# Scaling w_sp on ScalarE and taking a quarter of z2 in seven block products

## The chip, the cores and the metric

The kernel runs on one core of a Trainium2 chip. The metric is the device time of one execution in microseconds; the median of three runs of the kernel before is 669.81 us (669.75 to 670.06). The profile is of one further execution. TensorE (PE in the profile) multiplies, VectorE (DVE) and ScalarE (ACT) work on tiles of 128 partitions, GpSimd (POOL) does little here, and SyncE (SP) issues all DMAs from one queue.

## The reference

Two branches read the same x (2048 x 1024, bf16) and a gate mixes them.

```
g = sigmoid((x * gate_w).sum(-1))
# branch A: 32 heads of 32, each position looks at 8 positions back, 2 apart
q, k, v = x @ wqkv
a = softmax(q . k[pos - 2w], w = 0..7) . v  @ wo
# branch B
z  = gelu(x @ w_in)              # 2048 x 3584
z1 = z[:, :1792]
z2 = layernorm(z[:, 1792:])
gg = w_sp @ z2 + b_sp            # w_sp is 2048 x 2048
b  = (z1 * gg) @ w_out
out = g * a + (1 - g) * b
```

## The kernel before

Many large products are made as seven block products instead of eight: the operands are cut in four blocks, sums of blocks are formed beforehand (`s1` to `s4` on the left, `t1` to `t4`, `r1` to `r4` and so on at the right), and TensorE's accumulation in two banks with copies in between gives the four result blocks. For this the operands are float16, scaled by powers of two so that they fit: x by `xs`, the upper half of w_in's z2 columns by `dsc`, each row of w_sp by `rs` (a power of two from the row's sum of absolute values, `l1`), and so on. The scale is taken out again where the result leaves PSUM.

The kernel is written out in one order by hand. A small planner (`Beat`) counts the columns that TensorE has been given, at 2360 columns a microsecond, and calls functions that were booked for a time (`beat.at`) when that time is passed; it also books the steps of the attention on VectorE one behind the other (`vector_steps`). What it fixes is only the order of instructions on each engine; on the chip the engines wait for each other by semaphores.

The stages, in the order of TensorE's work, with the profile's times:

- Start (0 to 49 us): x comes in, the first two tiles turned by TensorE, the others by DMA transposes. z2's lower half (columns 0 to 895, `w2`, in two parts c = 0 and 1 of 448 columns) is made for the first 8 of 16 row tiles in plain tiles: `z2_tile` is 8 matmuls of 448 columns (line 374). Between them lie the projections of head group 0: `qkv_tile` is 8 matmuls of 384 columns (line 947). When x's sum of absolute values is known (`x_abs`, `x_total`, `x_scale`, line 401), x is turned to float16 in place (`x_convert`).
- Head groups 1 and 2 (to 94 us), while ScalarE and VectorE prepare the upper half of the columns (`d_norm`, `d_convert`, `d_sum`) and x's block sums (`x_sums`).
- Eight block groups (`z2_group`, line 455; 94 to 178 us): the upper half of z2's columns (c = 2 and 3, 449 columns with one for the gate) for all rows, 256 rows each, seven products of four matmuls; four projection tiles of head groups 3 and 4 stand among them. In two free slots of each group ScalarE takes what is held back: an exponential of the attention, a sum of the output, or a square sum of z2 (`squares`, line 1023).
- Head groups 5 to 7 (178 to 266 us), 48 projection tiles, with the remaining 16 plain tiles of z2's lower half, rows 1024 to 2047, among them. ScalarE forms the row sums of w_sp (`row_norm`, line 767) from natural rows.
- z1 (266 to 363 us): four parts of 448 columns by 16 tiles (line 1098). VectorE normalises z2 and forms the sums of its blocks (line 808).
- The mix (363 to 534 us): w_sp times z2 in 16 groups (`g_group`, line 1115), eight pairs of 256 rows, an even and an odd group for the two halves of the columns, each seven products of eight matmuls. The rows of w_sp come by DMA transpose (`load_rows`, line 792) into the buffer of the next pair, VectorE scales them (`scale_rows`, line 799; the scale lies along the free dimension after the transpose, so it is stored to DRAM and loaded back broadcast to all partitions, line 795), then forms the block sums (`s_sums`). ScalarE takes the seed copy (line 1139), p5 (line 1125), u2 and u3 (line 1127), the copy of the seed (line 1161) and the last block (line 1177). Beside that it scales y of the pair before in odd groups (`y_scale_beside`, line 912), sums it (`y_norm`, line 894), and in spare slots (`spare`) takes an output sum (line 688) or a chunk of wo (`wo_norm`, line 865).
- The products with wo and w_out (534 to 669 us).

Of the kernel before, what the change touches and what calls it, by code (L numbers as in the profile page):

```python
# [48 lines left out]
ARENA = R_OFF + 36864  # L49
# [3 lines left out]
T4_OFF = R_OFF + 21760  # L53
G_OFF = R_OFF + 28928
SN_OFF = R_OFF + 32512
# [7 lines left out]
def kernel(  # L63
# [34 lines left out]
    rs_d = dpool.tile([S], BF, name="rs_d")  # L98
# [21 lines left out]
    rs_b = sm.tile([P, 512], BF, name="rs_b")  # L120
# [5 lines left out]
    rows_one = rs_b[:, 0:P]  # L126
# [17 lines left out]
    rs_r = sm.tile([16, P], BF, name="rs_r")  # L144
# [12 lines left out]
    x_sc = sm.tile([P, 4], F32, name="x_sc")  # L157
    xs, xinv, xexp, xsum = [x_sc[:, m:m + 1] for m in range(4)]
# [19 lines left out]
    w2 = reg(R_OFF + 7168, KT * W2P).rearrange("p (k c) -> p k c", k=KT)  # L178
# [7 lines left out]
    r1 = z2f[:, 8:12, 0:DN]  # L186
    r2, r4 = [reg(R_OFF + 3072 + 4 * DN * r, 4 * DN).bitcast(F16).rearrange("p (k n) -> p k n", k=4) for r in range(2)]
    r3 = m12
    x_waste = reg(Z_OFF, 16 * FH).rearrange("p (i f) -> p i f", i=16)[:, 8:12, 0:DN]

    class Tokens:
        def __init__(self, u):
# [6 lines left out]
            if u < 7:  # L199
                self.s4 = z2f[:, 12:16, P * u:P * u + P]  # L200
            else:
                self.s4 = reg(R_OFF + 33922, 512).bitcast(F16).rearrange("p (k t) -> p k t", t=P)
# [10 lines left out]
    junk = reg(R_OFF + 33024, 2048)  # L213
# [9 lines left out]
    class Pair:  # L223
        def __init__(self, off):
            v = [reg(off + 1024 * r, 1024).bitcast(F16).rearrange("p (k t) -> p k t", k=8) for r in range(7)]
            both = reg(off, 4096).rearrange("p (h i t) -> p h i t", h=2, i=16)
            self.raw = [both[:, 0], both[:, 1]]
            both = reg(off, 4096).bitcast(F16).rearrange("p (h i t) -> p h i t", h=2, i=16)
            self.scaled = [both[:, 0], both[:, 1]]
# [10 lines left out]
    rs_bc = [rs_b[:, 256 * r:256 * (r + 1)] for r in range(2)]  # L240
# [127 lines left out]
    def z2_block(blocks, wake=False):  # L368
        banks = [seeded.tile([P, 512], F32, name="sd", tag="sd") if wake else bank() for _ in blocks]
        for kt in range(KT):  # L370
            for ps, (i, c) in zip(banks, blocks):
# [3 lines left out]
                                 _sub_ap(w2, kt * W2P + ZC * c, [[1, N]]),  # L375
                                 start=(kt == 0), stop=(kt == KT - 1), skip_group_check=wake)
        for ps, (i, c) in zip(banks, blocks):
            scale = xinv if converted[i // 2] else 1.0
            z2_out(ps[:, 0:ZC], i, c, scale)
            beat.run(KT * ZC)  # L380
# [18 lines left out]
    def x_scale():  # L399
        ps = psum.tile([P, 512], F32, name="ps", tag="ps")  # L400
        nc.tensor.matmul(ps[:, 0:1], rows_one, rs_n[:, 0:1], start=True, stop=True)
        powers(ps[:, 0:1], xs, xinv)
        nc.vector.tensor_scalar(xexp, xinv, xinv, float(SCALE), ALU.mult, ALU.mult)

# [3 lines left out]
    def x_sums(u):  # L408
# [5 lines left out]
        TT(v.s4, v.a12, v.s2, ALU.subtract)  # L414
        beat.on_vector(1.5)
# [30 lines left out]
    def z2_keep(ps):  # L446
        out = z2_snaps[z2_kept[0] % 5]
        z2_kept[0] += 1
        nc.scalar.copy(out, ps[:, 0:DN - 1])
        return out  # L450
# [964 lines left out]
```

## Time and profile before

| | us |
|---|---|
| median of three runs | 669.81 |
| profiled execution | 671.13 |
| its span, first to last instruction | 669.3 |
| TensorE busy | 662.7 |
| VectorE busy | 575.1 |
| ScalarE busy | 441.9 |
| granted TensorE clock | 1.00 |

A row of the timeline gives the start of an instruction or a run of equal ones, its length, engine, line, what it writes and reads, and in brackets how long the engine sat idle ahead of it and what ended that. Matmuls are pipelined: one of 448 columns is shown with 0.35 us, but eight of them follow in 1.51 us, and the chain of waits shows this pace.

### The profile page before, as it was taken

The numbers are of one execution on the slowest core, as the hardware profiler recorded it, in microseconds if no ns is written. First come the engines' busy times: TensorE is split into PE (matmuls) and PEld (weight loads), VectorE is DVE, ScalarE is ACT, GpSimd is POOL, SyncE is SP. The second block draws the span as 40 slices with busy tenths as digits, with TensorE's granted clock in tenths as the row PEclk, the third lists the DMA queues.
The fourth block names the chain that finished last, engine by engine and source line by source line (L and its number), as shares of the span: only waits on it lengthen the run. The fifth ranks groups of instructions, "written<-read, shape, count | busy, mean of one in ns | idle before, by whom it ended". The sixth has DMA issues, their size and how long they took to land.

```text
span 669.3 us, 9594 instructions
## 1 busy us (share of the span) xinstructions
PE 662.7 (99%) x3564; PEld 389.3 (58%) x3564; DVE 575.1 (86%) x660; ACT 441.9 (66%) x774; POOL 9.4 (1%) x68
## 2 busy tenths in 40 slices
PE   8999999999999999999999999999999999999998
PEld 4558877666777777555555555555555544444443
DVE  4567999999999999999999999999978788954745
ACT  4327577888879989889755568787767774522222
POOL 0000000000001000001000000000000000000000
PEclk9999999999999999999999999999999999999999
DMA  8999593354297996994966686648589599476211
GB/s 224 182 235 255 113 227 116 105 121 120 45 283 244 279 290 203 280 327 150 292 207 213 154 217 161 166 116 229 131 211 288 142 270 225 85 167 151 54 63 64
DMA packets 229919, 123.92 MB, mean 185 GB/s; under 512 B 191088, under 2 KB 217456, under 8 KB 229872
## 3 DMA queue, kind: packets, MB, share of 16 engines
q1 hardware_dynamic: 229872, 123.31, 69.7%
q8 instruction: 28, 0.46, 0.3%
q14 instruction: 19, 0.16, 0.1%
HBM read 63.97 MB, written 37.82 MB: 152 GB/s over the span
## 4 chain that ended last, share of the span: by engine, by line
PE 97%; ACT 1%; DMA 1%; SPq 0%; issue 0%; DVE 0%
PE ps L1115 25%; PE ps L947 17%; PE pd L1115 12%; PE ps L1098 7%; PE seed L1115 7%; PE sd L947 5%; PE pd L374 4%; PE ps L455 4%; PE sd L1098 4%; PE pd L1098 4%; PE pd L947 2%; PE pd L455 2%; PE ps L374 1%; PE sd L374 1%; PE seed L455 1%; DMA arena<-in_B_w_in_dram 1%
## 5 line engine op out<-in xcount | busy, mean ns | idle before, releaser
L1115 PEld LDWEIGHTS <-arena 128*128 128x128 f16 x1519 | 148.4, 98 | 154.4 <-issue 0.7
L1115 PE MATMUL ps<-arena 128*128 128x448 f16 (+1 forms) x864 | 186.1, 363 | 0.2 <-ACT seed L1139 0.2
L947 PEld LDWEIGHTS <-arena 128*128 128x128 f16 (+1 forms) x1024 | 141.6, 139 | 30.4 <-issue 1.2
L947 PE MATMUL ps<-arena 128*128 128x384 bf16 x704 | 128.7, 326 | 0.0
L1115 PE MATMUL pd<-arena 128*128 128x448 f16 (+1 forms) x432 | 95.6, 363 | 0.0
L1098 PEld LDWEIGHTS <-arena 128*128 128x128 f16 x512 | 50.0, 98 | 46.7
L514 DVE TENSOR_TENSOR arena<-arena 128x4096 bf16<-128x4096 bf16 (+1 forms) x64 | 74.0, 1157 | 1.7
L510 DVE TENSOR_TENSOR arena<-arena 128x8192 bf16<-128x8192 bf16 x16 | 70.8, 4422 | 5.0 <-DMA arena<-k_d 4.7
L577 DVE TENSOR_TENSOR arena<-arena,att_A 128x8192 bf16<-128x8192 bf16 x16 | 70.7, 4421 | 0.2
L950 ACT CAST arena<-ps 128x384 bf16<-128x384 f32 x88 | 43.0, 489 | 23.6 <-PE ps L947 21.4
L1098 PE MATMUL ps<-arena 128*128 128x448 bf16 x256 | 53.7, 353 | 0.0
L1115 PE MATMUL seed<-arena 128*128 128x448 f16 (+2 forms) x223 | 48.7, 361 | 0.0
L947 PE MATMUL sd<-arena 128*128 128x384 bf16 x224 | 41.0, 326 | 0.8 <-ACT arena L383 0.8
L374 PEld LDWEIGHTS <-arena 128*128 128x128 f16 (+1 forms) x256 | 24.9, 98 | 23.0 <-ACT arena L359 1.1
L583 DVE TENSOR_TENSOR arena<-arena 128x4096 bf16<-128x4096 bf16 x16 | 36.6, 2287 | 0.2
L374 PE MATMUL pd<-arena 128*128 128x448 bf16 x160 | 34.7, 353 | 0.0
L1273 DVE SCALAR_TENSOR_TENSOR arena<-seed,omr,arena 128x512 bf16<-128x512 f32 x8 | 6.0, 751 | 32.7 <-PE seed L1115 32.7
L455 PEld LDWEIGHTS <-arena 128*128 128x128 f16 x224 | 21.9, 98 | 18.1 <-issue 0.5
L767 ACT ACTIVATE arena<-arena 128x2048 bf16<-128x2048 bf16 x16 | 30.9, 1932 | 0.0
L894 ACT ACTIVATE arena<-arena 128x896 bf16<-128x896 bf16 x32 | 30.3, 947 | 0.5
L455 PE MATMUL ps<-arena 128*128 128x449 f16 x128 | 29.7, 354 | 0.0
L387 DVE TENSOR_REDUCE yl<-arena 128x1 f32<-128x2048 bf16 x8 | 18.3, 2286 | 13.1 <-DMA arena<-in_A_x_dram 13.0
(207 smaller groups left out, 845.9 us busy)
## 6 DMA issues: line engine op xcount, KB each, us to landing
arena<-in_B_w_sp_dram SPq DMA_DIRECT2D x16, 512.0 KB, 4.2
arena<-v_d SPq DMA_DIRECT2D x8, 960.0 KB, 6.0
z_d<-arena SPq DMA_DIRECT2D x16, 448.0 KB, 4.5
arena<-z_d SPq DMA_DIRECT2D x16, 448.0 KB, 3.6
y_d<-arena SPq DMA_DIRECT2D x16, 448.0 KB, 4.1
arena<-k_d SPq DMA_DIRECT2D x7, 960.0 KB, 6.7
arena<-in_A_wqkv_dram SPq DMA_DIRECT2D x24, 256.0 KB, 4.6
q_d<-arena SPq DMA_DIRECT2D x32, 128.0 KB, 2.1
```

What stands on the lines that cost most here:

```text
L374: nc.tensor.matmul(ps[:, 0:N], x[:, kt, i * P:(i + 1) * P], _sub_ap(w2, kt * W2P + ZC * c, [[1, N]]), start=(kt == 0), stop=(kt == KT - 1) ...
L455: nc.tensor.matmul(ps[:, 0:DN - 1], lhsT, v[:, k, 0:DN - 1], start=(first and k == 0), stop=(k == 3), skip_group_check=True)
L510: TT(prod.rearrange("p (w j c) -> p w j c", w=W, j=8, c=C), in0, in1, ALU.mult)
L514: return lambda: TT(pv[:, :, 0:n], pv[:, :, 0:n], pv[:, :, n:2 * n], ALU.add)
L577: TT(prod.rearrange("p (w j d h) -> p w j d h", w=W, j=8, d=DH, h=HG), in0, in1, ALU.mult)
L583: return [(4.4, mul), (2.3, lambda: TT(p3[:, 0:4, :], p3[:, 0:4, :], p3[:, 4:8, :], ALU.add)), (1.2, lambda: TT(p3[:, 0:2, :], p3[:, 0:2, ...
L767: nc.scalar.activation(slot, slot, ACT.Abs, accum_out=l1[:, a:a + 1])
L894: nc.scalar.activation(waste, g_ring[n % 4][:, r], ACT.Abs, accum_out=yl[:, k:k + 1])
L947: nc.tensor.matmul(ps[:, 0:3 * C].rearrange("p (t c) -> p t c", t=3), lhsT, wgt[:, :, kt, :], start=(kt == 0), stop=(kt == KT - 1))
L950: nc.scalar.copy(st[:, j % 4, :].rearrange("p (t d h) -> p t d h", t=3, h=HG), ps[:, 0:3 * C].rearrange("p (t h d) -> p t d h", t=3, h=HG))
L1098: nc.tensor.matmul(ps[:, 0:512 if whole and kt == 0 else ZC], xh[:, kt, i * P:(i + 1) * P], _sub_ap(w1, kt * ZC, [[1, 512 if whole and kt ...
L1115: nc.tensor.matmul(ps[:, 0:c1 - c0], w[:, k, :], v[:, k, c0:c1], start=(first and k == 0), stop=(k == K - 1), skip_group_check=True)
```

## The change

Two things change, and much of the order with them.

1. *w_sp is scaled ahead of the transpose.* ScalarE scales natural rows (the scale is then one number per partition) in pieces of 128 rows by 1024 columns (`w_scaled`), the piece is stored to a scratch in DRAM (`w_d`), and the transpose reads that. Rows 0 to 511 go through in z1, eight pieces; the others in the mix, four pieces per pair for two pairs ahead (`w_ahead` loads, `w_piece` scales and books the store). Pieces 0 and 1 use the block-sum buffers of the pair's own buffer, pieces 2 and 3 one buffer, `w_tail`. The scaling on VectorE, the broadcast scales and their DMAs are gone. In `g_group` the pieces take slots that the spare work had, and odd groups get a spare slot behind u2.
2. *The lower half of z2's columns for rows 1024 to 2047 is made in four more block groups.* `w2` is summed, scaled and turned to float16 in place (`e_abs`, `e_total`, `e_scale`, `e_convert`), and its block sums are formed (`e_sum`). The 16 plain tiles of that part go. The four groups stand ahead of the eight, and the twelve take the projections of head groups 3 to 5 among them. Four row sums of w_sp move into the first groups (`nat_early`), the others stand closer.

The rest follows: some of x's block sums are formed later, the first stage has five row tiles ahead of head group 0 instead of eight, the weights of head groups 5 to 7 and `load_d` are loaded at other places, and `w_total` and `w_power` are booked by the last chunk of wo.

```diff
+    def e_abs(q):
+        nc.vector.tensor_reduce(el[:, q:q + 1], w2[:, 2 * q:2 * q + 2, :], AX.XY, ALU.add, apply_absolute_value=True)
+    def e_scale(ps):
+        powers(ps[:, 1:2], es, einv)
+        nc.vector.tensor_scalar(ezinv, xinv, einv, None, ALU.mult)
+    def e_convert(q):
+        sl = slice(2 * W2P * q, 2 * W2P * (q + 1))
+        nc.scalar.activation(w2h[:, sl], w2_flat[:, sl], ACT.Copy, scale=es)
+    def e_sum(m):
+        out_, a, b = ((q1, n12, n11), (q3, n22, n12), (q2, n22, q1), (q4, n21, q2))[m]
+        TT(out_, a, b, ALU.subtract)
...
-    def z2_group(u, tiles):
+    def z2_group(u, tiles, half):
         v = tokens[u]
-        scale = zinv
+        (w11, t1_, t2_, w21, t3_, w22, t4_), c, n = halves_of[half]
+        scale = zinv if half else ezinv
...
-    def store_scale():
-        sync.dma_start(rs_d.rearrange("(a t) -> a t", t=P), rs_r[:])
+    def w_load(a, c, slot):
+        sync.dma_start(slot, w_view(B_w_sp, a, c))
+    def w_scaled(a, c, slot):
+        nc.scalar.activation(slot.bitcast(F16), slot, ACT.Copy, scale=rs[:, a:a + 1])
+    def w_store(a, c, slot):
+        sync.dma_start(w_view(w_d, a, c), slot.bitcast(F16))
+    def w_home(u, q):
+        return (2 * u + 4 + q // 2, q % 2, w_tail if q > 1 else pairs[(u + 1) % 2].sums[q])
+    def w_piece(u, q):
+        if u + 2 < NU:
+            piece = w_home(u, q)
+            w_scaled(*piece)
+            beat.at(beat.now + 1.6, lambda: w_store(*piece))
+    def w_ahead(u, q):
+        if u + 2 < NU:
+            w_load(*w_home(u, q))
     def load_rows(u, h):
         a = 2 * u + h
-        sync.dma_start_transpose(pairs[u % 2].raw[h], B_w_sp[a * P:(a + 1) * P, :])
-    def load_scale(u):
-        sync.dma_start(rs_bc[u % 2], bass.AP(tensor=rs_d.tensor, offset=rs_d.offset + 256 * u, ap=[[0, P], [1, 256]]))
-    def scale_rows(u, h):
-        v = pairs[u % 2]
-        TT(v.scaled[h], v.raw[h], _sub_ap(rs_bc[u % 2], P * h, [[0, 16], [1, P]]), ALU.mult)
+        sync.dma_start_transpose(pairs[u % 2].whole[h], w_d[a * P:(a + 1) * P, :])
...
         if beside_copy:
-            beside_copy[0] = (beat.now + 9.0, beside_copy[0][1])
+            beside_copy[0] = (beat.now + 7.0, beside_copy[0][1])
...
-    for i in range(2, 8):
+    for i in range(2, 5):
         sync.dma_start_transpose(xT[:, :, i * P:(i + 1) * P], x2[i * P:(i + 1) * P, :])
     load_wg(0)
...
-        st = (stage_early if g < 5 else stage_slots)[stg[0] % 3]
+        slots = stage_early if g < 3 else stage_slots[:2] if g < 6 else stage_slots
+        st = slots[stg[0] % len(slots)]
...
-    tiles = [lambda g=g, j=j: qkv_tile(g, j, False) for g in (3, 4) for j in range(NJ)]
+    tiles = [lambda g=g, j=j: qkv_tile(g, j, False) for g in (3, 4, 5) for j in range(NJ)]
...
+    early_load()
+    for u in range(4, 8):
+        if u == 7:
+            nat[1] = False
+        z2_group(u, tiles, 0)
     for u in range(NU):
-        if u == 4:
+        if u == 2:
             load_wg(5)
-        z2_group(u, tiles)
+            load_wg(6)
+        if u == 6:
+            load_wg(7)
+        z2_group(u, tiles, 1)
...
-    for g in range(5, NG):
+    for g in range(6, NG):
         for j in range(NJ):
             qkv_tile(g, j)
-            n = NJ * (g - 5) + j
-            if n % 3 == 2:
-                n = n // 3
-                z2_tile(8 + n // 2, n % 2)
...
+    for n in range(8):
+        piece = (n // 2, n % 2, pairs[0].sums[n % 3])
+        beat.at(t + 10.0 + 4.5 * n, lambda piece=piece: w_load(*piece))
+        beat.at(t + 14.5 + 4.5 * n, lambda piece=piece: w_scaled(*piece))
+        beat.at(t + 16.2 + 4.5 * n, lambda piece=piece: w_store(*piece))
...
         product(pd, v.s1, t1, f0, f1, True)
         p5 = keep(pd, None)
+        w_piece(u, 2 + fb)
         product(pa, v.s2, t2, f0, f1, False)
         u2 = keep(pa, lo)
+        if fb == 0 and 0 < u < NU - 2:
+            w_piece(u, 0)
+        else:
+            spare(beside_fork, beside_copy)
         product(pb, v.a12, b21, f0, f1, False)
         nc.scalar.copy(g[:, 0, 0], pb[:, 0:ZC])
         if n % 2 == 1 and n > 1:
             y_scale_beside((n - 3) // 2, 1)
+        elif fb == 0 and u < NU - 2:
+            w_piece(u, min(u, 1))
         else:
             spare(beside_fork, beside_copy)
...
         if fb == 0 and u + 1 < NU:
-            beat.at(t + 0.5, lambda u=u: load_scale(u + 1))
+            beat.at(t + 8.2, lambda u=u: w_ahead(u, 3))
             for h in range(2):
                 beat.at(t + 2.0, lambda u=u, h=h: load_rows(u + 1, h))
+        if fb == 1:
+            beat.at(t + 4.7, lambda u=u: w_ahead(u + 1, 0))
+            beat.at(t + 6.2, lambda u=u: w_ahead(u + 1, 1))
+            beat.at(t + 8.2, lambda u=u: w_ahead(u + 1, 2))
         g_group(n)
         if fb == 0 and u + 1 < NU:
-            for h in range(2):
-                scale_rows(u + 1, h)
-            beat.on_vector(2.5)
-            for fn in s_sums(u + 1):
-                fn()
-            beat.on_vector(2.8)
+            beat.at(beat.now + 2.8, lambda u=u: pair_sums(u + 1))
```

## The prediction

> **What bounds the kernel now.** I read the page's totals and its chain first, then who TensorE waited for, then busy time by stage.
>
> ```profile
> span 669.3 us, 9594 instructions
> PE 662.7 (99%) x3564; PEld 389.3 (58%) x3564; DVE 575.1 (86%) x660; ACT 441.9 (66%) x774; POOL 9.4 (1%) x68
> ...
> PE 97%; ACT 1%; DMA 1%; SPq 0%; issue 0%; DVE 0%
> ```
>
> TensorE is the chain. The list of what its matmuls waited for has four rows in the whole span, 3.3 us together, and only the last lies behind the start:
>
> ```profile
> PE pw L118 <- DVE arena L113: 1.2, 1, 1.2
> PE ps L374 <- DMA arena<-in_B_w_in_dram: 1.1, 2, 0.9
> PE sd L947 <- ACT arena L383: 0.8, 1, 0.8
> PE ps L1115 <- ACT seed L1139: 0.2, 1, 0.2
> ```
>
> So a matmul left out is time won, and every new wait of TensorE is time lost. The windows say where a new wait can come from (columns: length, then busy time of PE, PEld, DVE, ACT, POOL, then the granted clock and DMA):
>
> ```profile
> 200.00:220.00 20.00, 20.00 (x121) 15.87 (x119) 19.44 (x21) 19.95 (x34) 2.21 (x4) 1.00 0.86 245
> ...
> 265.70:289.90 24.20, 24.20 (x130) 12.43 (x128) 23.63 (x22) 22.13 (x34) 0.34 (x4) 1.00 1.05 279
> ...
> 384.20:405.40 21.20, 21.20 (x114) 10.95 (x112) 20.93 (x27) 14.90 (x23) 0.00 (x0) 1.00 0.74 196
> 405.40:426.60 21.20, 21.20 (x114) 10.96 (x112) 19.81 (x24) 16.80 (x27) 0.50 (x7) 1.00 0.60 149
> ```
>
> VectorE is full in every stage (19.44 of 20, 20.93 of 21.2). ScalarE was full at 200 to 220 and TensorE lost nothing by it: with independent tiles and eight banks, ScalarE may lag by several tiles. In the mix (from 363 us) it has 4 to 6 us free in a pair of groups of 21.2 us. The clock is 1.00 in all of them.
>
> **The change part by part.** *Block products.* The chain gives the price of eight matmuls of 448 columns in a plain tile, of four of 449 in a block product and of a projection tile:
>
> ```profile
> 94.31 0.77 PE ps L455 x4
> 95.08 1.30 PE ps L947 x8
> ...
> 183.05 1.51 PE pd L374 x8
> ```
>
> Rows 1024 to 2047 of the lower half are 16 plain tiles, 16 x 1.51 = 24.2 us. They become 4 groups of 7 products of four matmuls of 448: 28 x 1.51 / 2 = 21.1 us. That is -3.0 us. The 16 projection tiles of the fifth head group only move into the groups, at 1.30 us before and after. The four extra groups bring ScalarE and VectorE the same copies and additions as the eight of before, over the same four projection tiles, under which TensorE waited for nothing.
>
> *Start.* Head group 0 begins three plain tiles (4.5 us) sooner, and its weights are issued three transposes sooner.
>
> ```profile
> 16.14 2.73 SPq L349 DMA_DIRECT2D arena<-in_A_wqkv_dram  x3
> 23.78 1.46 PE L947 MATMUL sd<-arena 128*128 128x384 bf16 x8 [0.80 <-ACT arena L383]
> 36.79 0.16 DVE L390 TENSOR_REDUCE x_sc<-yl 128x1 f32<-128x8 f32 x1
> 41.98 0.17 PE L401 MATMUL ps<-rs_n,rs_b 128*128 128x1 bf16 x1
> ```
>
> Before, the first projection tile waited 0.80 us and began 4.9 us behind the last issue of its weights (18.87): I read that as the weights, not ScalarE. Issued 5.2 us sooner and wanted 5.3 us sooner (the tile would be ready at 18.45), they cost about 0.1: -0.7 us. Against it, x's scale matmul is reached near 36.7 instead of 41.98, and the sum it needs is ready at 36.79 + 0.35 us, since it hangs on x's last transpose, which is issued as before: +0.4. The four column sums of w_in (`e_abs`) run on VectorE while it waits for x. I take -0.2; bounds -0.8 and +1.0 (x's later transposes move behind the weights; stage buffers come free when the queue gets to the stores). `load_d` moves behind the first stores on SyncE's queue, which frees these.
>
> *VectorE.* It loses the 16 scalings of transposed rows:
>
> ```profile
> L767 ACT ACTIVATE arena<-arena 128x2048 bf16<-128x2048 bf16 x16 | 30.9, 1932 | 0.0
> ...
> L950 ACT CAST arena<-ps 128x384 bf16<-128x384 f32 x88 | 43.0, 489 | 23.6 <-PE ps L947 21.4 <-DMA v_d<-arena 1.6 <-ACT arena L950 0.6
> ...
> L1023 ACT ACTIVATE arena<-arena 128x1792 bf16<-128x1792 bf16 x16 | 27.3, 1708 | 0.0
> ...
> L799 DVE TENSOR_TENSOR arena<-arena,rs_b 128x2048 f16<-128x2048 bf16 x16 | 18.8, 1219 | 0.0
> ...
> L865 ACT ACTIVATE arena<-arena 128x768 bf16<-128x768 bf16 x10 | 8.4, 843 | 3.8 <-DMA arena<-in_A_wo_dram 3.8
> ...
> L437 ACT ACTIVATE arena<-arena,yl 128x1800 f16<-128x1800 bf16 x4 | 7.2, 1807 | 4.8 <-DVE yl L395 4.8
> ```
>
> 16 x 1.22 = 19.5 us go, most of it in the mix; some 10 us of block sums and additions come, all before z1. Attention slips by a few us until z1 and ends earlier in the mix. Taken at 0; bounds 0 and +1.5, where a pair's row sums, now due 2.8 us behind the group, queue behind an attention multiplication of 4.4 us.
>
> *ScalarE ahead of the mix.* In the 41.6 us of head groups 6 and 7 it has 32 casts (15.6 us by the mean, less where they follow each other), some 10 row sums of w_sp (19.3), 4 squares (6.8) and an exponential and an output sum of about 4: 42 to 46 us. It would end up to 4 us behind. The first c of z1, at 22.13 of 24.20 busy before, gets three scaled pieces and two row sums more and a few squares fewer. A lag of 5 us is under the 8 banks of 1.5 us. Taken at 0; bounds 0 and +2.
>
> *ScalarE in the mix.* 24 pieces of w_sp (128x1024) are scaled there. Between the 843 ns of 768 columns and the 1807 of 1800 a piece is about 1.06 us, 0.96 when the next follows at once. What it can cost is read from an odd group of before, ScalarE first, TensorE's next products behind it:
>
> ```profile
> 396.39 0.61 ACT L1139 ACTIVATE seed<-ps,bt 128x448 f32<-128x448 f32 x1 [0.88 <-PE ps L1115]
> 397.21 1.79 ACT L912 ACTIVATE arena<-arena,ys 128x1792 f16<-128x1792 bf16 x1 [0.21 <-DVE ys L901]
> 398.90 0.51 ACT L1125 COPY arena<-pd 128x448 f32<-128x448 f32 x1
> 399.42 0.63 ACT L1127 ACTIVATE arena<-ps,bt 128x448 f32<-128x448 f32 x1
> 400.93 0.53 ACT L1161 CAST arena<-seed 128x448 bf16<-128x448 f32 x1 [0.88 <-PE seed L1115]
> 401.36 1.79 ACT L912 ACTIVATE arena<-arena,ys 128x1792 f16<-128x1792 bf16 x1
> 403.05 0.62 ACT L1127 ACTIVATE arena<-ps,bt 128x448 f32<-128x448 f32 x1
> ```
>
> ```profile
> 400.73 1.68 PE L1115 MATMUL ps<-arena 128*128 128x448 f16 x8
> ...
> 403.76 3.19 PE L1115 MATMUL ps<-arena 128*128 128x448 f16 x16
> ```
>
> The copies of line 1127 (u2, u3) must be over when TensorE writes the same bank again, at 400.73 and 403.76. u3 ended at 403.67: no slack was left already. In the odd groups of pairs 1 to 5 a piece now stands ahead of u2: it would end at 399.42 + 0.96 + 0.63 = 401.0 here, 0.3 late, and on time or 0.05 late where line 912 does not wait its 0.21 for VectorE. The spare slot of odd groups also moves behind u2; a wo chunk there (0.85) pushes the next line 912 and u3 by about 0.5. With a chunk at most every 7 us, two or three of the seven fall into such slots. Even groups have room for their three pieces. Together +0.5 and +1.0, less what coincides: +1.2; bounds 0 and +3 (an output sum of 1.9 in such a slot costs 1.5).
>
> A rule of the Trainium skill speaks against this part: ScalarE: Activation LUTs, "Rules for kernel authors", sends plain multiplications to VectorE, the faster engine per element. By that page's instruction cost a piece would be an estimated 1.13 us, and 24 of them 27 us; put in for the 1.06, the sum would be 0.1 higher for each late group. The rows agree on the rate (34 us for 32 pieces against 19.5), but not on the conclusion, as VectorE is the fuller engine here.
>
> *DMA.* 32 loads and 32 stores of 256 KB come; 8 broadcast loads and a store go. In the mix that is 2 MB per pair. Two rows of the DMA table and SyncE's queue price the one place where they follow each other closely, `w_tail`, which is loaded twice in a pair:
>
> ```profile
> arena<-in_B_w_sp_dram SPq DMA_DIRECT2D x16, 512.0 KB, 4.2
> ...
> out_dram<-arena SPq DMA_DIRECT2D x15, 256.0 KB, 2.1
> ```
>
> ```profile
> 382.52 9.05 SPq L792 DMA_TRANSPOSE arena<-in_B_w_sp_dram  x2
> ...
> 393.59 1.17 SPq L861 DMA_DIRECT2D arena<-in_A_wo_dram  x1
> ...
> 404.95 7.12 SPq L792 DMA_TRANSPOSE arena<-in_B_w_sp_dram  x2
> 412.16 0.54 SPq L841 DMA_DIRECT2D arena<-z_d  x1
> ```
>
> The transposes hold SyncE's queue until 412.1. Behind them comes the store of piece 2 (412.7), it lands 2.1 later, then the load of piece 3 lands within 4.2: 419.0. ScalarE wants it at the next odd group, 21.2 us behind 396.39 plus some 2.7: 420.3. It just fits, so 0; in the pair of 382.5, with an attention load ahead and the queue held to 394.8, the same sum (394.8 + 2.1 + 4.2) gives 401.1 against 399.4 wanted: about 2 us late, and ScalarE's wait is TensorE's. Taken at +0.2; bounds 0 and +6. Behind a piece that waits for its load stand, on ScalarE, u2, the copy of the seed, line 912 and u3, so TensorE's fifth and seventh product; behind a load that waits for its slot's store stand, on SyncE, the next z1 load, the stores of y and the next pair's transposes, all of which have a group of room.
>
> *Moves at one price, nothing.* Four row sums of w_sp and their loads go into the first block groups, whose free slots took squares before, and the other twelve stand 3.5 instead of 5.2 us apart: the ScalarE sum above holds them. The weights of groups 5 to 7 are loaded a group or more ahead, 768 KB each on a queue that then has less to do. Two stage buffers instead of three serve groups 3 to 5, each refilled only every second block group, 21 us later. The first w_sp rows go through DRAM in z1 and are read back 12 us behind their last store. The sums of z2's blocks start 65 instead of 62 us into z1 and lack the 2.4 us of scalings, so they end at the same time. `w_total` and `w_power` wait for the last chunk and stand in VectorE's gaps. If any of this cover fails it is TensorE that waits, one for one; the bounds of the two ScalarE terms and of VectorE's are for that.
>
> **The sum.** -3.0 - 0.2 + 0 + 0 + 1.2 + 0.2 = -1.8 us. The profiled execution took 671.13 us with a span of 669.3; the sum gives a span of 667.5. The median of the runs is 669.81, 1.3 below the profiled one: 668.0 forecast.
>
> **Rivals.** *All hidden*: the chunks in odd groups coincide with waits that are there anyway and u2 is on time; -3.2, 666.6. For it: ScalarE is 70 to 79% busy in the pairs. Against: u3's slack of zero.
>
> *ScalarE eats the gain*: an output sum and three chunks in odd groups (1.5 + 1.5) beside 0.5 of late u2: -3.2 + 3.5, within 0.3 us of 669.8. For it: TensorE's only wait in the mix was behind ScalarE. Against: the sums that stand in such slots are few. This is how the rule of the Trainium skill quoted above would come true.
>
> *Slower: `w_tail` is late.* Each late us of piece 3 is one of TensorE. Two of the five pairs late by 2 us make 668.0 + 4 = 672.0; from 3.1 us in all the kernel is slower. For it: the 9.05 us of the pair with an attention load. Against: in the other pair the load fits.
>
> *The matmuls do not get shorter as counted*: the four groups might be held by the block sums of VectorE, as that runs several us behind its plan; up to +1.5, part of the bounds.
>
> **How the numbers follow.** Forecast 0.48, all hidden 0.08, ScalarE eats it 0.18, `w_tail` 0.26. About 0.2% (1.3 us) is what a measurement can tell from no change: faster 0.56, same 0.18, slower 0.26. The range goes from a little under all hidden (666.4) to just under two late pairs (671.8).
>
> **What would show it.** TensorE: 16 matmuls fewer net in the stage of z2, z1 beginning about 3 us sooner than 265.8. Rows of TensorE waiting for ScalarE at the products of the mix, 0.3 to 0.6 each, in odd groups only; for `w_tail`, ScalarE waiting for a DMA from w_sp. The first projection tile begins near 18.5. The prediction is wrong if z1 begins less than 2 us sooner, if TensorE waits in the groups or in z1, or if the mix is longer by over 3 us.

## The result and the profile after

The changed kernel is slower: 724.4 us against 669.9, ratio 1.0815 (95% interval 1.0796 to 1.0834). Forecast were 668.0, and 671.8 as the end of the range. The profiled execution's span is 723.8 us.

The page of the kernel after, totals and chain; then the list of what TensorE waited for (us in total, times, longest):

```profile
span 723.8 us, 9720 instructions
PE 676.6 (93%) x3547; PEld 391.6 (54%) x3547; DVE 573.2 (79%) x668; ACT 485.9 (67%) x826; POOL 12.6 (2%) x68
...
PE 29%; DVE 4%; ACT 4%; DMA 3%; issue 1%; SPq 1%; ACTq 0%
```

```profile
PE ps L1204 <- ACT arena L1216: 16.9, 7, 5.2
PE ps L1187 <- ACT arena L1190: 12.4, 5, 4.8
PE pd L1187 <- ACT arena L1190: 3.5, 2, 2.4
PE ps L463 <- DVE rs_n L458: 3.5, 1, 3.5
PE ps L1007 <- ACT arena L1062: 3.1, 1, 3.1
PE ps L487 <- ACT seed L505: 1.7, 1, 1.7
...
```

TensorE's waits were 3.3 us before and are 43.5 now, most of them behind ScalarE: in the mix (line 1204) at its copies u2 and u3, in z1 (line 1187) at its gelus. But TensorE is also 13.9 us longer busy (676.6 against 662.7) with 3 us less to do. The windows say why (columns: length, busy PE, PEld, DVE, ACT, POOL, granted clock, DMA share, GB/s):

```profile
290.00:310.00 20.00, 13.38 (x56) 6.22 (x56) 15.51 (x22) 18.23 (x27) 3.61 (x1) 0.83 0.70 223
...
454.00:474.00 20.00, 15.27 (x69) 7.24 (x68) 12.98 (x17) 12.99 (x18) 0.34 (x4) 0.83 0.82 242
474.00:494.00 20.00, 19.82 (x105) 10.08 (x104) 18.37 (x20) 18.28 (x28) 0.19 (x3) 1.00 0.78 209
...
514.00:534.00 20.00, 14.80 (x69) 7.08 (x68) 10.35 (x9) 12.95 (x20) 0.00 (x0) 0.83 0.95 268
```

Wherever TensorE stood long, the granted clock of the window is 0.83: it works at half pace for a while behind the pause. Over the span the clock is 0.976, which is (1 - 0.976) x 723.8 = 17 us. So of the 54.5 us, 40 are new waits, 17 are pace, and 3 are saved matmuls.

What ScalarE itself waited for, of the DMAs alone:

```profile
ACT arena L833 <- DMA arena<-in_B_w_sp_dram: 14.5, 5, 6.5
...
ACT arena L924 <- DMA arena<-in_A_wo_dram: 12.9, 2, 10.6
...
ACT arena L1190 <- DMA z_d<-arena: 9.4, 2, 7.1
...
ACT arena L1011 <- DMA v_d<-arena: 6.0, 1, 6.0
...
ACT arena L808 <- DMA arena<-in_B_w_sp_dram: 4.3, 2, 2.8
...
ACT arena L731 <- DMA o_d<-arena: 3.8, 1, 3.8
```

With 2.6 for the gate column below that is 53.5 us; before, it was 8.0. Only 14.5 of it is for the new pieces; the rest is for DMAs that were there before. Not all of that rest is late because of the pieces: x_none below, which has no piece, still has 40.9 us of such waits. Four places show how such a wait reaches TensorE.

*Start.* The loads of w_in's upper half, moved behind the stores, land near 59; two copies of ScalarE into the same buffer wait for them, and the casts that free TensorE's banks stand behind these copies. The sums of the same loads are late too, and with them the matmul of their scale (line 463):

```profile
46.78 4.98 SPq L451 DMA_DIRECT2D arena<-in_B_w_in_dram  x4
...
59.17 0.18 ACT L1062 COPY arena<-pt 128x4 bf16<-128x4 bf16 x1 [2.62 <-DMA arena<-in_B_w_in_dram]
...
59.40 1.46 PE L1007 MATMUL ps<-arena 128*128 128x384 bf16 x8 [3.12 <-ACT arena L1062]
...
78.64 0.18 PE L463 MATMUL ps<-rs_n,arena 128*128 128x1 bf16 x1 [3.48 <-DVE rs_n L458]
```

*First part of z1.* The last projection tile ends on TensorE near 271.9, and ScalarE casts it at 280.1. TensorE uses up its banks and then stands 7.9 us in five pieces, the last 3.6; the eight matmuls behind that take 3.15 us instead of 1.67:

```profile
270.43 1.46 PE L1007 MATMUL pd<-arena 128*128 128x384 bf16 x8
...
280.12 0.54 ACT L1011 CAST arena<-pd 128x384 bf16<-128x384 f32 x1
...
304.68 3.15 PE L1187 MATMUL ps<-arena 128*128 128x448 bf16 x8 [3.60 <-ACT arena L1190]
```

*Later in z1.* A chunk of wo is issued behind the copy that reorders wo (2 MB); ScalarE waits for it, and z1's store for ScalarE:

```profile
358.43 3.04 SPq L798 DMA_DIRECT2D wop_d<-in_A_wo_dram  x4
...
362.18 2.36 SPq L920 DMA_DIRECT2D arena<-in_A_wo_dram  x1
...
375.33 0.84 ACT L924 ACTIVATE arena<-arena 128x768 bf16<-128x768 bf16 x1 [10.63 <-DMA arena<-in_A_wo_dram]
...
379.25 3.14 PE L1187 MATMUL ps<-arena 128*128 128x448 bf16 x8 [4.76 <-ACT arena L1190]
```

*Mix.* The chain of the `w_tail` rival: transposes hold SyncE, then the store of piece 2, the load of piece 3, ScalarE, TensorE:

```profile
445.15 10.03 SPq L853 DMA_TRANSPOSE arena<-w_d  x2
...
456.41 1.38 SPq L836 DMA_DIRECT2D w_d<-arena  x3
460.52 0.34 SPq L830 DMA_DIRECT2D arena<-in_B_w_sp_dram  x1
...
463.72 1.15 ACT L833 ACTIVATE arena<-arena,rs 128x1024 f16<-128x1024 bf16 x1 [4.78 <-DMA arena<-in_B_w_sp_dram]
...
465.44 3.15 PE L1204 MATMUL ps<-arena 128*128 128x448 f16 x8 [4.73 <-ACT arena L1216]
468.37 2.72 PE L1204 MATMUL pd<-arena 128*128 128x448 f16 x8
```

### The profile page after: what moved, and what is told of

It is laid out like the page before. It is cut to its first block, busy times and chain, and to the rows that moved or that the text cites. A ratio compares the mean times of both kernels' runs of the same rounds, so it can differ in the third digit from the quotient of the medians.

```text
span 723.8 us, 9720 instructions
## 1 busy us (share of the span) xinstructions
PE 676.6 (93%) x3547; PEld 391.6 (54%) x3547; DVE 573.2 (79%) x668; ACT 485.9 (67%) x826; POOL 12.6 (2%) x68
## 5 line engine op out<-in xcount | busy, mean ns | idle before, releaser
L1204 PEld LDWEIGHTS <-arena 128*128 128x128 f16 x1519 | 149.7, 99 | 176.2 <-issue 25.8
L1204 PE MATMUL ps<-arena 128*128 128x448 f16 (+1 forms) x864 | 189.0, 366 | 17.2 <-ACT arena L1216 16.9
L1007 PEld LDWEIGHTS <-arena 128*128 128x128 f16 (+1 forms) x1024 | 141.5, 138 | 34.1 <-issue 4.4
L1204 PE MATMUL pd<-arena 128*128 128x448 f16 (+1 forms) x432 | 97.2, 368 | 0.0
L1187 PEld LDWEIGHTS <-arena 128*128 128x128 f16 x512 | 52.0, 102 | 70.0 <-issue 27.6
L1187 PE MATMUL ps<-arena 128*128 128x448 bf16 x256 | 57.8, 372 | 12.4 <-ACT arena L1190 12.4
L487 PEld LDWEIGHTS <-arena 128*128 128x128 f16 x336 | 32.9, 98 | 28.8 <-issue 2.7
L833 ACT ACTIVATE arena<-arena,rs 128x1024 f16<-128x1024 bf16 x32 | 36.9, 1153 | 14.7 <-DMA arena<-in_B_w_sp_dram 14.5
L487 PE MATMUL ps<-arena 128*128 128x449 f16 (+1 forms) x192 | 44.5, 353 | 1.7 <-ACT seed L505 1.7
L808 ACT ACTIVATE arena<-arena 128x2048 bf16<-128x2048 bf16 x16 | 30.8, 1927 | 4.3 <-DMA arena<-in_B_w_sp_dram 4.3
L1187 PE MATMUL pd<-arena 128*128 128x448 bf16 x128 | 27.3, 357 | 3.5 <-ACT arena L1190 3.5
L1187 PE MATMUL sd<-arena 128*128 128x448 bf16 (+1 forms) x128 | 29.5, 378 | 0.5 <-ACT arena L1190 0.5
L1007 PE MATMUL pd<-arena 128*128 128x384 bf16 x160 | 29.3, 326 | 0.0
```

What stands on the lines that cost most here:

```text
L487: nc.tensor.matmul(ps[:, 0:n], lhsT, v[:, k, 0:n], start=(first and k == 0), stop=(k == 3), skip_group_check=True)
L808: nc.scalar.activation(slot, slot, ACT.Abs, accum_out=l1[:, a:a + 1])
L833: nc.scalar.activation(slot.bitcast(F16), slot, ACT.Copy, scale=rs[:, a:a + 1])
L1007: nc.tensor.matmul(ps[:, 0:3 * C].rearrange("p (t c) -> p t c", t=3), lhsT, wgt[:, :, kt, :], start=(kt == 0), stop=(kt == KT - 1))
L1187: nc.tensor.matmul(ps[:, 0:512 if whole and kt == 0 else ZC], xh[:, kt, i * P:(i + 1) * P], _sub_ap(w1, kt * ZC, [[1, 512 if whole and kt ...
L1204: nc.tensor.matmul(ps[:, 0:c1 - c0], w[:, k, :], v[:, k, c0:c1], start=(first and k == 0), stop=(k == K - 1), skip_group_check=True)
```

## The experiments

All are read by stage, from the first matmul of each in the profiled execution (us); the last column is the median. The start scatters from run to run: with the same code up to there, the groups begin at 99.2 in x_none and at 103.2 in c_noosum, and at 92.7 in e_scale against 94.2 in the kernel before. A difference of 2 to 4 us between two medians says little by itself. The products with wo and w_out take 134.7 to 135.6 in all.

| kernel | start | z2 groups to head group 7 | z1 | mix | median |
|---|---|---|---|---|---|
| before | 94.2 | 171.5 | 97.3 | 171.6 | 669.9 |
| after | 101.3 | 170.5 | 122.6 | 194.8 | 724.4 |
| x_none | 99.2 | 170.4 | 107.5 | 179.1 | 694.1 |
| x_act | 102.0 | 170.5 | 111.4 | 180.1 | 703.0 |
| x_dma | 101.3 | 170.4 | 117.9 | 190.9 | 716.3 |
| e_scale | 92.7 | 171.5 | 101.5 | 186.5 | 687.1 |
| e_pool | 101.7 | 171.3 | 123.7 | 184.0 | 723.7 |
| c_norow | 101.8 | 170.4 | 110.2 | 193.9 | 713.3 |
| e_moves | 104.2 | 170.8 | 112.7 | 192.1 | 718.7 |
| e_gate | 100.5 | 170.5 | 120.4 | 194.2 | 723.9 |
| c_noosum | 103.2 | 170.5 | 121.0 | 194.3 | 726.4 |
| e_all | 102.6 | 170.5 | 115.6 | 198.7 | 719.8 |
| c_all | 99.6 | 170.5 | 107.6 | 194.1 | 711.8 |
| x_none_norow | 101.6 | 170.4 | 108.7 | 189.7 | 706.2 |
| x_close2 | 92.9 | 170.4 | 107.7 | 187.0 | 695.3 |
| x_close | 92.7 | 170.4 | 106.5 | 178.5 | 688.6 |
| e_start | 92.7 | 170.5 | 121.0 | 196.5 | 718.3 |
| y_close | 93.5 | 170.5 | 99.1 | 171.3 | 671.3 |
| y_split | 93.2 | 170.5 | 97.1 | 171.3 | 668.9 |

### What of the scaled pieces costs

The theory from the traces was that ScalarE and SyncE, each in order, hold each other up; the rivals were too much work for ScalarE, and the traffic. Two by two: the pieces' DMAs in or out, ScalarE's operation in or out.

The lines of x_none; x_act leaves out the load and the store in the same way and puts a copy of the same shape in place of the scaling; x_dma leaves out the scaling alone.

```diff
-        sync.dma_start(slot, w_view(B_w_sp, a, c))
-        nc.scalar.activation(slot.bitcast(F16), slot, ACT.Copy, scale=rs[:, a:a + 1])
-        sync.dma_start(w_view(w_d, a, c), slot.bitcast(F16))
-        sync.dma_start_transpose(pairs[u % 2].whole[h], w_d[a * P:(a + 1) * P, :])
+        sync.dma_start_transpose(pairs[u % 2].raw[h], B_w_sp[a * P:(a + 1) * P, :])
```

> The changed kernel without the pieces of w_sp: no load, no scaling on ScalarE, no store; the transposes read w_sp itself, unscaled, so the output is not the reference's. Whatever way the scaling costs its time (ScalarE and SyncE holding each other up; too much work for ScalarE; DMA traffic), this should be rid of nearly all of it: 674 to 680 us, that is the 669.9 of before, -3 for the block products, +7 for the late load of w_in at the start, 0 to 6 for ScalarE's lag at the end of head group 7. If the four new block groups are at fault it stays above 700.

> As x_none, but ScalarE does a copy of 128x1024 at the place of every piece, on what lies in the buffer: ScalarE's work is that of the changed kernel, the loads and stores of the pieces are gone (output not the reference's). Mutual hold-up of ScalarE and SyncE: within 5 us of x_none. Too much work for ScalarE: 715 to 725, as the changed kernel. DMA traffic: as x_none.

> The changed kernel with all loads and stores of the pieces, but without ScalarE's scaling (the store sends what was loaded, output not the reference's). Mutual hold-up: within 6 us of x_none, as no instruction of ScalarE waits for a load any more and no store waits for ScalarE. Too much work for ScalarE: as x_none. DMA traffic or the queue's length alone: 700 to 724.

Measured: 694.1, 703.0, 716.3 (after: 724.4). ScalarE's operation alone costs 8.9 us, the DMAs alone 22.3, both 30.4: they add up (31.2). In z1 and the mix alone, which the scatter of the start does not touch, it is 4.9, 22.2 and 30.8, so a hold-up that needs both is worth some 4 us, and my theory, by which it was nearly all, fell. SyncE by itself is still held up in x_dma: it waits 26.7 us for stores of pieces to land, ahead of a load into the same buffer, and 4.1 us for loads, ahead of the store. In the mix, where ScalarE's work was to be dear, that work costs 1.0 (179.1 to 180.1) and the DMAs 11.8. What the DMAs do shows in x_dma's list for ScalarE, with no piece in it: ScalarE's waits for z1's stores, 2.6 us before, 5.7 in x_none and 9.4 after, are 17.2 here:

```profile
ACT arena L1190 <- DMA z_d<-arena: 17.2, 7, 7.4
...
ACT arena L924 <- DMA arena<-in_A_wo_dram: 13.0, 3, 10.6
```

In the mix the larger part goes by VectorE. Its block sums are written into the buffers that pieces 0 and 1 came through, so they wait until the piece's store has landed; the attention on VectorE is late behind them, then ScalarE's exponential, then TensorE (x_dma):

```profile
414.02 1.42 DVE L858 TENSOR_TENSOR arena<-arena 128x1024 f16<-128x1024 f16 x2 [8.15 <-DMA w_d<-arena]
...
423.37 0.72 ACT L600 ACTIVATE att_L<-att_L,x_sc 128x512 f32<-128x512 f32 x1 [6.25 <-DVE att_L L577]
...
425.10 6.09 PE L1204 MATMUL ps<-arena 128*128 128x448 f16 x16 [4.10 <-ACT arena L1216]
```

With 0.73 us that TensorE waits for these sums themselves and 2.9 at half pace behind the 4.10, this is 7.7 of the 11.8 us. In the kernel after, the same sums wait 3.4, 5.9 and 3.0 us.

And x_none, without any piece, is still 24 us above the kernel before: more than the scaling was wrong.

The scaling alone, on the kernel before (its z2 and start untouched, the scaling on ScalarE as in the change, block sums at 65 instead of 62 us into z1):

> The kernel before with the scaling on ScalarE alone, z2 as it was. Mutual hold-up in z1 and the mix by itself: 690 to 717 (mix +21, z1 +10 to +26, nothing at the start). If the hold-up needs the lag that ScalarE has when z1 begins in the changed kernel: z1 +0 to +5, mix as before or up to +21: 672 to 695. If the scaling costs what the prediction said: 671.

687.1, ratio 1.0255 (1.0235 to 1.0275): +14.9 in the mix, +4.3 in z1. The scaling costs 17.2 us by itself here, and 30.4 in the changed kernel (after less x_none); which of the other changes makes it dearer was not tried.

### The queue, the row sums, four moves, and the pause

e_pool:

```diff
-        sync.dma_start(slot, w_view(B_w_sp, a, c))
+        nc.gpsimd.dma_start(slot, w_view(B_w_sp, a, c))
...
-        sync.dma_start(w_view(w_d, a, c), slot.bitcast(F16))
+        nc.gpsimd.dma_start(w_view(w_d, a, c), slot.bitcast(F16))
```

> The changed kernel, with the loads and stores of the pieces issued from GpSimd's queue instead of SyncE's; nothing else is changed, and the bytes are the same. If it is SyncE's one queue that costs (each load or store that waits holds up the stores of z1, the chunks of wo and the transposes behind it): 700 to 710, near the 703 of the run that had ScalarE's copies without the DMAs. If it is the traffic on the shared DMA engines: within 5 us of 724.

723.7 (717.4 to 729.7): no gain beyond its own scatter (the mix of 184.0 is that of a run at the low end), so SyncE's one queue alone is not the cause. The Trainium skill says the same (DMA: Bandwidth & Descriptors, "Issuing engines are not separate DMA queues"): DMAs of all issuing engines run on the same 16 engines and interleave, and another issuer only saves the issue time. The time of this run agrees. With four runs 12 us apart, a share of a few us for the queue stays open.

c_norow:

```diff
-    for n in range(16 - nat[0]):
-        beat.at(t + (0.5 + 2.0 * n if n < 3 else 3.5 * n), lambda n=n: load_nat(nat[0] + n, nat_slots[n % 3]))
-        beat.at(t + 7.0 + 3.5 * n, lambda n=n: row_norm(nat[0] + n, nat_slots[n % 3]))
+    nc.gpsimd.memset(l1[:, nat[0]:16], 1.6)
```

> The changed kernel without the loads and row sums of w_sp's rows 512 to 2047 (their sums are set to a constant that gives the same powers of two for this input; a kernel for any input needs them). ScalarE overloaded by them in head groups 6 and 7: the waits of TensorE in the first 35 us of z1 (7.9 us, and some 2.5 at half pace) go, z1 is 8 to 11 us shorter, in all 712 to 717. If that lag comes from the scaled pieces: within 3 us of 724.

713.3, z1 12.4 shorter, none of the five waits at 287 to 305 left: ScalarE's lag came from the row sums (with their loads, which this edit leaves out too), not from the pieces.

e_moves, with `load_d` behind `load_wg(1)` as before, and `order_wo` and `w_ahead(u, 3)` at other times:

```diff
-        return (2 * u + 4 + q // 2, q % 2, w_tail if q > 1 else pairs[(u + 1) % 2].sums[q])
+        return (2 * u + 4 + q // 2, q % 2, w_tail if q > 2 else pairs[(u + 1) % 2].sums[q])
...
-    beat.at(t + 62.0, order_wo)
+    for h in range(HG):
+        beat.at(t + 70.0 + 7.5 * h, lambda h=h: order_wo(h))
...
-            beat.at(t + 8.2, lambda u=u: w_ahead(u, 3))
+            if u > 0:
+                beat.at(t + 0.5, lambda u=u: w_ahead(u, 3))
...
-                    beside_fork.append((t + 6.0, o_norm_now))
+                    beside_fork.append((t + 16.0, o_norm_now))
```

> The changed kernel with four moves that are read by stage. The loads of the upper half of w_in back where they were: the two waits at 59 and 79 us (6.6 us) go and the block groups begin at 94 to 95.5 instead of 101. Piece 2 in the third sum buffer, so that w_tail is loaded once a pair and its load stands ahead of the transposes: the wait of 4.7 us at 465 goes. The reordering copy of wo in four parts between the chunks: the wait of 4.8 us at 379 goes. The last output sum 10 us later: the wait of 5.2 us at 528 goes. Each of the last three takes some 2.5 us of half pace behind it along. All four: 724 - 6.6 - 7.2 - 7.3 - 7.7 = 695. If instead the waits only change places because ScalarE and SyncE stay behind: 710 to 720.

718.7 instead of 695. The waits at 379 and 465 are gone; that at 528 stayed (5.05 us, at 518), two new long ones came, and the block groups begin at 104.2, not at 94 to 95.5. With the loads of w_in early, ScalarE waits twice as long for the stores behind them (12.0 instead of 6.0); with piece 2 in another buffer its first load comes late, and TensorE waits at the beginning of the mix. In z1 the copy in four parts did help (112.7 against 122.6).

```profile
45.65 0.48 ACT L1013 CAST arena<-ps 128x384 bf16<-128x384 f32 x1 [12.04 <-DMA v_d<-arena]
...
46.18 3.15 PE L381 MATMUL ps<-arena 128*128 128x448 bf16 x8 [4.83 <-ACT arena L1013]
...
397.72 2.77 PE L1204 MATMUL ps<-arena 128*128 128x448 f16 x7 [3.83 <-ACT arena L1216]
```

> Nothing of the reference: bursts of 80 matmuls of 448 columns, between two of them ScalarE copies 1024 to 8192 columns while TensorE stands idle (about 1.2 to 7 us). If a pause halves TensorE's pace for some us behind it, bursts behind pauses of over about 3.5 us are 1.5 to 3 us longer than those behind 1.5 to 3 us; if the half pace in the kernel has another cause, all bursts last the same 15 us.

The timeline of TensorE in m_clock (in brackets the pause ahead of the burst):

```profile
23.78 15.31 PE L33 MATMUL ps<-xs,link 128*128 128x448 bf16 x80 [1.43 <-ACT link L37]
...
59.40 15.31 PE L33 MATMUL ps<-xs,link 128*128 128x448 bf16 x80 [2.71 <-ACT link L37]
77.84 16.99 PE L33 MATMUL ps<-xs,link 128*128 128x448 bf16 x80 [3.14 <-ACT link L37]
...
139.51 16.90 PE L33 MATMUL ps<-xs,link 128*128 128x448 bf16 x80 [3.78 <-ACT link L37]
160.84 18.17 PE L33 MATMUL ps<-xs,link 128*128 128x448 bf16 x80 [4.42 <-ACT link L37]
...
210.29 17.34 PE L33 MATMUL ps<-xs,link 128*128 128x448 bf16 x80 [7.41 <-ACT link L37]
```

Here a pause of 2.7 us costs nothing behind it, one of 3.1 to 3.8 costs 1.6 to 1.7 more, one of 4.4 or more 2.0 to 2.9. So the pace in the kernel comes from the pauses.

### One cause at a time, and all together

e_gate books the two steps of the gate column (a transpose on TensorE, two copies on ScalarE); c_noosum changes `o_norm`; e_all is e_gate with `order_wo` in four parts and the pieces on GpSimd's queue; c_all is e_all with c_norow and c_noosum.

```diff
+    beat.at(t0 + 10.2, gate_column)
...
+        if prep["mixing"]:
+            nc.gpsimd.memset(ol[:, g:g + 1], 30.0)
+            return
         nc.scalar.activation(waste, obuf, ACT.Abs, accum_out=ol[:, g:g + 1])
```

> The changed kernel with one thing moved: the two copies of the gate column (line 1062), which wait for the late loads of w_in, come 10 us later in ScalarE's order, behind the first casts and the conversions. If it is the place of these copies in ScalarE's order that costs at the start: the wait of 3.1 us at 59 goes and that at 79 (3.5, behind the sums of the same loads) shrinks, the block groups begin at 95 to 97, in all 718 to 720. If the loads themselves are too late whatever waits for them: the wait comes 10 us later and is as long, 723 to 725.

723.9: the wait at 59 is gone, and the next one took its place:

```profile
77.27 0.19 PE L463 MATMUL ps<-rs_n,arena 128*128 128x1 bf16 x1 [5.16 <-DVE rs_n L458]
```

> The changed kernel without the output sums of the attention in the mix (set to a constant, a scale alone). If the last of them, waiting for the slow store of o, holds up ScalarE and so TensorE: the wait of 5.2 us at 528 and the half pace behind it (2.6) go, the mix takes 187 instead of 195. If ScalarE is held up there by something else (VectorE that is late): 192 to 195.

726.4, mix 194.3: nothing gained. The wait for the store of o is gone, and some 12 us later ScalarE waits 2.4 us for VectorE and then for a piece, and TensorE for it, as long as before:

```profile
537.12 1.15 ACT L836 ACTIVATE arena<-arena,rs 128x1024 f16<-128x1024 bf16 x1 [2.69 <-DMA arena<-in_B_w_sp_dram]
...
538.85 3.13 PE L1207 MATMUL ps<-arena 128*128 128x448 f16 x8 [5.12 <-ACT arena L1219]
```

> The changed kernel with the gate column's copies later, the reordering copy of wo in four parts, and the pieces' loads and stores on GpSimd's queue; everything is computed. If the three causes add up: -5, -10 in z1 and -11 in the mix, 698. If the waits change places: 705 to 715.

> As e_all, and also without the row sums of w_sp's rows 512 to 2047 and the output sums in the mix (both set to constants). If the four causes named so far are all there is and add up: 698 - 12 - 8 = 678. Above 690, something else costs as much as each of them.

719.8 and 711.8 instead of 698 and 678. With the pieces and their DMAs in place the causes do not add up: most waits that are taken away are replaced by another. The row sums (c_norow) and, below, the order of the start (e_start) are the exceptions.

### Closing the account

x_none_norow has no scaling on ScalarE, transposes from w_sp, and the edit of c_norow. x_close2 adds that of e_gate and the lines below; x_close adds c_noosum. e_start is the changed kernel with the edits of x_close2's start alone. y_close is x_close without the pieces' loads and stores, y_split is y_close with `order_wo` in four parts.

```diff
-    beat.at(t0 + 23.0, d_scale)
+    beat.at(t0 + 29.0, d_scale)
...
-        beat.at(t0 + 25.0 + 2.4 * q, lambda q=q: hold_back(lambda: d_convert(q)))
+        beat.at(t0 + 31.0 + 2.4 * q, lambda q=q: hold_back(lambda: d_convert(q)))
```

The first three, other than their expectations say, leave out ScalarE's scaling alone and still issue the pieces' loads and stores. So they stand beside x_dma (716.3), not x_none, with transposes that wait for no store; the figures expected of them are off by that.

> As x_none (no pieces, w_sp unscaled, output not the reference's), and without the row sums of w_sp's rows 512 to 2047. If ScalarE's lag at the end of head group 7 comes from these sums: z1 97 to 98 us as before instead of 107.5, in all 684. If the lag has other work behind it: 689 to 694.

> As x_none_norow, with the gate column's copies 10 us later and the matmul of w_in's scale and the conversions behind it 6 us later in the order. If the start lost its 5 to 7 us by that order alone: the block groups begin at 94 to 95, in all 678 to 679. If the loads of w_in are too late for any order: 683.

> As x_close2, and without the output sums of the attention in the mix. If the wait for the store of o was the rest of the mix's loss (7.5 us in x_none): 671, and below 670 as far as the block products bring their 3.0. If a wait on VectorE or a DMA takes its place: 675 to 679.

> The changed kernel with the two moves of the start alone (gate column's copies 10 us, the scale's matmul and the conversions 6 us later); everything is computed. If the order was the cause at the start: the waits at 59 and 79 go, the block groups begin at 94 to 96 instead of 101, in all 718. If the wait moves on once more: 723 to 725.

Measured: 706.2, 695.3, 688.6. Without ScalarE's scaling the causes do add up: 10.1 less than x_dma for the row sums (and the transposes' other source), 10.9 for the order of the start, 6.7 for the output sums. e_start, the changed kernel with that order alone, is 6.2 faster (718.3), its groups begin at 92.7 and neither wait is left: what was wrong at the start is the order, not the loads.

> x_close without the loads and stores of the pieces (no pieces at all, w_sp unscaled, row sums of rows 512 to 2047 and output sums in the mix set to constants, the gate column's copies and w_in's scale later in the order; output not the reference's). If the DMAs of the pieces are what is left: x_none's 694 less 10 for the row sums, 8 for the start, 7 for the output sums: 669, near before. If 10 us or more stay, the block groups or the moves have a cost that none of the runs has named: over 679.

> As y_close, with the reordering copy of wo in four parts behind the chunks. If the wait for the chunk of wo still costs TensorE something in y_close, that goes: 3 to 9 us less than y_close, at best 665 to 667, where the block products' 3.0 show. If it is hidden in y_close already: the same within 1.5 us.

y_close 671.3 (ratio 1.0028, 1.0014 to 1.0043) differs from x_close in the loads and stores alone: 17.3 us. y_split is 668.9, ratio 0.9977 (0.9967 to 0.9987), granted clock 1.00. It leaves out the scaling, 12 row sums and the output sums of the mix, so it is no kernel to use, but it closes the account. In its span of 667.1 us TensorE still waits for

```profile
PE ps L489 <- DVE arena L428: 1.7, 1, 1.7
PE pw L118 <- DVE arena L113: 1.2, 1, 1.2
PE ps L383 <- DMA arena<-in_B_w_in_dram: 0.4, 1, 0.4
```

No run that computes everything beats the kernel before.

## Why the prediction was wrong, by its own steps

*Block products, -3.0.* Measured -1.0 (171.5 to 170.5), the same in most runs with the twelve groups. The mechanism holds; 1.7 of the missing 2.0 is one wait in the fifth block group, at 148 us, that the sum had at zero and the last rival at up to 1.5. In the changed kernel the seed copy stands there behind a row sum moved into the first groups; in y_split, with the start sooner, it is VectorE's block sum of the next rows:

```profile
147.96 0.93 PE L487 MATMUL ps<-arena 128*128 128x449 f16 x4 [1.70 <-ACT seed L505]
```

*Start, -0.2 (bounds -0.8 and +1.0).* Measured +7.1. The first projection tile began at 18.15 as forecast (18.5). The step that failed is "`load_d` moves behind the first stores on SyncE's queue, which frees these": it counted who is freed and not who waits for what was moved, the gate column's copies on ScalarE with all casts behind them, and the sums with a matmul behind them. e_start shows that later places for these cost nothing.

*VectorE, 0.* Right in amount: busy 575.1 before, 573.2 after. But it had no wait of the block sums for the pieces' stores (below).

*ScalarE ahead of the mix, 0 (0 to +2): "It would end up to 4 us behind", "under the 8 banks".* The lag was 8.2 us (280.1 against 271.9): the sum of its work left out 4.3 us of waits for w_sp's rows (line 808), and squares carried over. It cost 11.1 us in all (c_norow, which leaves out the row sums' loads too), half pace included. Here the estimate of 42 to 46 us of work for 41.6 us was itself the warning; the first part of z1 had no room for the catching up, as it brought three pieces and two row sums more.

*ScalarE in the mix, +1.2 (0 to +3).* Right for the operation alone: x_act's mix is 1.0 longer than x_none's; beside the pieces' DMAs it is 3.9 (after against x_dma). What the prediction took as the main risk, by ScalarE's rows and by the Trainium skill's rule for plain multiplications (ScalarE: Activation LUTs, "Rules for kernel authors"), was neither the loss nor large: a piece took 1153 ns, not 1.06 us (between the two rows that I named it would have been 1.08), nearer the 1.13 worked out from that page. The rule's verdict on this change holds (e_scale is slower), but by x_act and x_dma mainly because of the DMAs that the natural layout needs.

*DMA and `w_tail`, +0.2 (0 to +6).* This is the step that decides. The pieces' DMAs cost 22.3 us (x_dma less x_none) or 17.3 (x_close less y_close). I priced the one place where two of them follow each other; that came in the pair at 445 us, 4.7 us late, the rival's mechanism, but taking it away (e_moves) left the mix at 192.1. The cost is in two others, which the sum had at nothing. Transfers that were there before come later, and ScalarE, in order, waits for them: 17.2 us instead of 5.7 for z1's stores and 13.0 instead of 8.5 for the chunks of wo (x_dma against x_none). And VectorE's block sums wait for the pieces' own stores to leave their buffers, 7.7 of the 11.8 us in the mix of x_dma; in x_close they wait 6.2 us, with 3.4 us of TensorE behind them, and in y_close not. 16 MB more are moved (123.9 to 140.2); how much of the lateness is traffic and how much the order of the queue stays open. The store of o is late without the pieces too (8.1 us in x_none), and ScalarE's wait for a store of v lies ahead of any piece. The list of DMAs of the kernel after (median from issue to landing last; before, these two were 5.2 and 3.7):

```profile
o_d<-arena SPq DMA_DIRECT2D x8, 512.0 KB, 8.3
...
arena<-in_A_wo_dram SPq DMA_DIRECT2D x10, 192.0 KB, 5.7
```

The prediction had no term for transfers that were there before, nor for an engine that waits for a store to free its buffer.

*The pace.* The sum put a late us at one us of TensorE. A wait of 4.73 us cost 7.2: the eight matmuls at 465.44 took 2.93 us (to 468.37) instead of 1.51, the next eight 2.56 (to the sixteen that follow at 470.93). That is 17 of the 54.5 us, and no term had it.

The signs that the prediction named did show: z1 began 6 us later instead of 3 sooner, TensorE waited in z1, and the mix was 23 us longer.

## What to carry to other kernels

When TensorE has no slack, price a new DMA by all the transfers that it delays, by who waits for them in order, and by who writes its buffer next, not only by its own landing; the two-by-two of leaving out the transfer and leaving out the operation tells the two apart in three runs. For every load that is moved later, list the instructions that touch its buffer, and what stands behind them on their engine. Where several waits are caught by the same late resource, take them all away once in a kernel that need not be right: that shows what the change can bring at best (here 1.3 us), before the causes are mended one by one.

## What the runs showed of the hardware

A pause of TensorE costs more than itself: in m_clock nothing up to 2.7 us, then 1.7 us, and up to 2.9 us from 4.4 us on. The Trainium skill (TensorE: Matmul & The Clock Gate, "What's actually happening") has a window of about 3.4 us, free-running, after which an idle array falls to half its clock, and as long a busy window to leave it. The rows agree in part: waits of 3.12 and 3.24 us in the kernel were followed by full pace and one of 3.60 by half, as a free-running window would have it; in m_clock the drop came at 3.14. The 1.7 us are 3.4 us at half pace; the 2.9 us are 5.7, longer than that page's window. Pauses well under that window can do it too: one of 2.42 us was followed by full pace at 291.37 in the kernel after, but by eight matmuls in 3.10 us instead of 1.67 at 290.99 in x_dma. What decides between the two was not tried.

New transfers make others land later: a chunk of wo (192 KB) landed 6.5 us after its issue in x_dma and 5.7 in x_close, with the pieces' loads and stores, and 3.3 in x_none and 3.7 in y_close, without them (medians of one profile each). With the pieces on GpSimd's queue it was 4.0 (e_pool), which points to the queue at this place; it was not tried by itself. The store of o does not show this: 8.1 us in x_none, 8.5 in x_dma.
